# Attention loads in four transfers of 64 partitions from the nineteenth chunk on

## The chip, the cores and the metric

The kernel runs on one core of a Trainium2 chip. The metric is the device time of one execution in microseconds. Three runs of the kernel before took 819.7, 819.75 and 819.98 us; the median is 819.75 us. Its profile comes from one further execution.

## The reference

Three layers, in float32. First a decaying linear attention over 4 batches, 8 heads, 768 steps and a head size of 64:

```
state = gamma * state + outer(k[t], v[t])
y[t]  = scale * (q[t] @ state)
```

The result, 3072 tokens by 512 features, goes through `h = (x @ w1) * (x @ w2) @ w3`, `x = h @ w_out` with an inner width of 1024, and then through `h = max(x @ w1, x @ w2, x @ w3)`, `x = h @ w_out` with an inner width of 768.

## The kernel before, in words

The attention works in chunks of 128 steps: 6 chunks in each of 4 batches, 24 in all. For a chunk, TensorE multiplies k by q for each head (line 360, the scores), VectorE multiplies the scores by a mask into a buffer `a` (line 365), GpSimd multiplies v by decay factors in place (line 350, `scale_v`), and TensorE adds two parts into one PSUM bank: the state of earlier chunks times q (line 373) and the masked scores times the scaled v (line 382, `attn_av`). Line 393 adds k times v to the state. VectorE moves the result out with the output's decay factors (line 400). VectorE also copies the decay factors of each pair of chunks (line 343), and GpSimd waits for that copy.

`seq` sets the order: chunks go in pairs, one of each of two batches. Chunks 0 to 11 belong to the batches 0 and 1, chunks 12 to 23 to the batches 2 and 3. While the pair i, i+1 is in hand, the scores, masks and scaled v of the pair i+2, i+3 are made (`scores_ahead`).

A chunk arrives in one of six buffers `ck0` to `ck5`, each of 128 partitions by 4 rows of 512 floats: row 0 is q and row 1 is k with features on partitions (heads of even place on partitions 0 to 63, of odd place on 64 to 127), rows 2 and 3 are k and v with steps on partitions. `load_half(i, 0)` loads rows 0 and 1 and `load_half(i, 1)` rows 2 and 3, each by one transfer on SP's queue (line 327), 4 KB on each of 128 partitions, 512 KB. In the last chunk of a batch the second transfer is row 3 alone, 256 KB. At the end of each pair four loads for the pair six chunks ahead are written, so the loads of chunks 18 to 23 stand in the pairs that begin with 12, 14 and 16. A transfer waits for its buffer to be free and for the semaphore that it uses: the program has eight for transfers and takes them in turn, so a transfer waits until the eighth before it has landed. The order is written out by hand; no scheduler moves it.

Behind the attention, SP stores `op` buffers (line 539) and loads weights (line 93), and TensorE begins the first expert layer (lines 573 to 575).

Of the kernel before, what the change touches and what calls it, by code (L numbers as in the profile page):

```python
# [15 lines left out]
P = 128  # L16
# [3 lines left out]
CPB = S // C  # L20
# [27 lines left out]
def fused_kernel(ctx: ExitStack, tc: tile.TileContext, ck, w12, w3t, wo1, w123, wo2, mask, gout, gch, kdec, out):  # L48
    nc = tc.nc
# [261 lines left out]
    def half(hh):  # L311
        return slice(64 * hh, 64 * hh + 64)

    seq = [(2 * g + z, j) for g in range(2) for j in range(CPB) for z in range(2)]
    last = len(seq) - 1

# [3 lines left out]
    def cks(i):  # L320
        return ck_t[i % NCK]

    def load_half(i, z):
        if i <= last:
            b, j = seq[i]
            o = 3 if z and j == CPB - 1 else 2 * z
            nc.sync.dma_start(out=cks(i)[:, o:2 * z + 2, :], in_=ck[b * CPB + j, :, o:2 * z + 2, :])

    def bank4(k, n=NP):
        return bank[k].rearrange("p (n c) -> p n c", n=n)  # L330
# [87 lines left out]

    with tc.manual_schedule():
        load_half(0, 0)  # L420
        nc.scalar.dma_start(out=kdec_sb, in_=kdec)
        load_half(1, 0)
        nc.scalar.dma_start(out=mask_sb, in_=mask)
        load_half(0, 1)
        load_half(1, 1)
        nc.vector.memset(warm_sb, 0.0)
# [124 lines left out]
        for g in range(KF // GA):  # L551
            for n in range(NB):
                blk = g * NB + n
                sets = sets_b(blk)
                for q in range(7):
# [13 lines left out]
                    for p in range(GA):  # L569
# [32 lines left out]
                        z = p if blk > NB else 2 * q + p // 2  # L602
# [3 lines left out]
                    z = s - 7 * (NB - 1) - LAG  # L606
# [121 lines left out]
        for s in range(XS):  # L728
            n, r = divmod(s, 14)
# [11 lines left out]
            for m in range(2):  # L741
                ps = bank[(4 if n % 2 == 0 else 0) + (2 if which == "b" else 0) + m]
                o = slice(m * P, (m + 1) * P)
# [184 lines left out]
        for s in range(7 * NB):  # L928
            n, q = divmod(s, 7)
# [9 lines left out]
            for r in range(2):  # L939
                ps = o_sets[n % 2][which][r]  # L940
                o = slice(r * P, (r + 1) * P)
# [87 lines left out]
```

## Time and profile before

| | |
|---|---|
| time, median of three runs | 819.75 us |
| time of the profiled execution | 818.71 us |
| its span, first to last instruction | 816.4 us |
| TensorE busy in the span | 805.8 us |
| DMA, mean over the span | 302 GB/s |

The span is what the rows below count from. The profiled execution took 2.3 us more than its span. Busy time of an engine isn't what the kernel waits for: a wait matters where the chain of work that ends last runs through it. The profile gives each idle stretch of an engine a releaser, the one that came last by the profile's own times; "issue" stands where it shows none.

### The profile page before, as it was taken

The numbers are of one execution on the slowest core, as the hardware profiler recorded it, in microseconds if no ns is written. First come the engines' busy times: TensorE is split into PE (matmuls) and PEld (weight loads), VectorE is DVE, ScalarE is ACT, GpSimd is POOL, SyncE is SP. The second block draws the span as 40 slices with busy tenths as digits, with TensorE's granted clock in tenths as the row PEclk, the third lists the DMA queues.
The fourth block names the chain that finished last, engine by engine and source line by source line (L and its number), as shares of the span: only waits on it lengthen the run. The fifth ranks groups of instructions, "written<-read, shape, count | busy, mean of one in ns | idle before, by whom it ended". The sixth has DMA issues, their size and how long they took to land.

```text
span 816.4 us, 12177 instructions
## 1 busy us (share of the span) xinstructions
PE 805.8 (99%) x4648; PEld 672.6 (82%) x4648; DVE 631.4 (77%) x795; ACT 388.2 (48%) x589; POOL 74.6 (9%) x93
## 2 busy tenths in 40 slices
PE   8999999999999999999999999999999999999998
PEld 8888888888888888888888888888888888888886
DVE  3799898989598988779799839994565565688793
ACT  2442545463336454557577545453334334434642
POOL 2443000000011111001010000000000000000000
PEclk9999999999999999999999999999999999999999
DMA  9997598789999984686789798989998699956522
GB/s 346 406 408 309 212 363 342 294 336 327 371 334 416 361 327 181 217 305 214 266 300 364 260 345 308 365 297 406 409 324 304 239 336 352 321 214 216 205 104 78
DMA packets 69961, 246.55 MB, mean 302 GB/s; under 512 B 6416, under 2 KB 6544, under 8 KB 69904
## 3 DMA queue, kind: packets, MB, share of 16 engines
q1 hardware_dynamic: 48672, 165.97, 53.8%
q10 hardware_dynamic: 21232, 79.81, 27.2%
q8 instruction: 37, 0.61, 0.3%
q14 instruction: 20, 0.16, 0.0%
HBM read 163.97 MB, written 81.79 MB: 301 GB/s over the span
## 4 chain that ended last, share of the span: by engine, by line
PE 93%; DVE 0%; issue 0%; ACT 0%; ACTq 0%
PE bank L872 11%; PE bank L873 10%; PE bank L874 10%; PE bank L575 9%; PE bank L574 9%; PE bank L573 9%; PE bank L746 5%; PE bank L747 5%; PE bank L748 5%; PE bank L944 4%; PE bank L945 4%; PE bank L943 3%; PE bank L662 2%; PE bank L661 2%; PE bank L663 2%; PE abank L382 1%
## 5 line engine op out<-in xcount | busy, mean ns | idle before, releaser
L573 PE MATMUL bank<-op,w 128*128 128x512 f32 x336 | 130.8, 389 | 0.0
L575 PE MATMUL bank<-op,w 128*128 128x512 f32 x336 | 130.7, 389 | 0.0
L574 PE MATMUL bank<-op,w 128*128 128x512 f32 x336 | 130.7, 389 | 0.0
L872 PE MATMUL bank<-op,w 128*128 128x512 f32 x330 | 128.5, 389 | 0.0
L874 PE MATMUL bank<-op,w 128*128 128x512 f32 x330 | 128.4, 389 | 0.0
L873 PE MATMUL bank<-op,w 128*128 128x512 f32 x330 | 128.4, 389 | 0.0
L126 POOL TENSOR_SCALAR dec<-dec 128x512 f32<-128x512 f32 x64 | 46.6, 729 | 554.4 <-ACT dec L124 520.5
L573 PEld LDWEIGHTS bank<-op,w 128*128 128x128 f32 x336 | 63.1, 188 | 13.3 <-issue 0.2
L574 PEld LDWEIGHTS bank<-op,w 128*128 128x128 f32 x336 | 63.1, 188 | 13.2
L575 PEld LDWEIGHTS bank<-op,w 128*128 128x128 f32 x336 | 63.1, 188 | 12.9
L872 PEld LDWEIGHTS bank<-op,w 128*128 128x128 f32 x330 | 61.9, 188 | 13.5 <-ACT bank L877 0.5
L874 PEld LDWEIGHTS bank<-op,w 128*128 128x128 f32 x330 | 61.9, 188 | 13.0
L873 PEld LDWEIGHTS bank<-op,w 128*128 128x128 f32 x330 | 61.9, 188 | 12.6
L748 PE MATMUL bank<-op,w 128*128 128x512 f32 x168 | 65.4, 389 | 0.0
L746 PE MATMUL bank<-op,w 128*128 128x512 f32 x168 | 65.4, 389 | 0.0
L747 PE MATMUL bank<-op,w 128*128 128x512 f32 x168 | 65.4, 389 | 0.0
L156 ACT ACTIVATE dec<-stg 128x512 int32<-128x512 uint32 x49 | 33.1, 676 | 52.2 <-DVE stg L149 45.8
L147 DVE TENSOR_SCALAR dec<-dec 128x512 int32<-128x512 int32 x64 | 27.0, 422 | 22.7 <-POOL dec L126 22.7
L124 ACT ACTIVATE dec<-stg 128x512 f32<-128x512 f32 x49 | 32.6, 664 | 12.7 <-DMA stg<-in_w_dram 6.5
L885 DVE TENSOR_TENSOR m<-m,bank 128x512 f32<-128x512 f32 x34 | 23.3, 684 | 19.5 <-PE bank L874 18.9
L944 PE MATMUL bank<-w,wo 128*128 128x512 f32 x96 | 37.4, 390 | 0.0
L945 PE MATMUL bank<-w,wo 128*128 128x512 f32 x96 | 37.4, 389 | 0.0
(216 smaller groups left out, 1581.7 us busy)
## 6 DMA issues: line engine op xcount, KB each, us to landing
op<-opsp ACTq DMA_DIRECT2D x53, 1024.0 KB, 8.1
opsp<-op SPq DMA_DIRECT2D x34, 1024.0 KB, 5.7
ck<-in_ck_dram SPq DMA_DIRECT2D x44, 512.0 KB, 10.1
fsp<-C SPq DMA_DIRECT2D x24, 512.0 KB, 4.8
op<-opsp SPq DMA_DIRECT2D x10, 1024.0 KB, 6.0
hsp<-m SPq DMA_DIRECT2D x32, 256.0 KB, 6.0
stg<-in_w_dram SPq DMA_DIRECT2D x15, 512.0 KB, 9.3
U<-fsp SPq DMA_DIRECT2D x14, 512.0 KB, 5.9
```

What stands on the lines that cost most here:

```text
L126: nc.gpsimd.tensor_scalar(out=df, in0=df, scalar1=MAX_HI, scalar2=MIN_HI, op0=ALU.min, op1=ALU.max)
L573: nc.tensor.matmul(ps, wh, x[:, 0, k, :], start=first and k == 0 and not seeded, stop=False, skip_group_check=True)
L574: nc.tensor.matmul(ps, wh, x[:, 1, k, :], start=False, stop=False, skip_group_check=True)
L575: nc.tensor.matmul(ps, wl, x[:, 0, k, :], start=False, stop=k == 1, skip_group_check=True)
L746: nc.tensor.matmul(ps, wh, x[:, 0, k, :], start=first and kk == 0 and k == 0, stop=False, skip_group_check=True)
L747: nc.tensor.matmul(ps, wh, x[:, 1, k, :], start=False, stop=False, skip_group_check=True)
L748: nc.tensor.matmul(ps, wl, x[:, 0, k, :], start=False, stop=kk == 1 and k == 1, skip_group_check=True)
L872: nc.tensor.matmul(ps, wh, x[:, 0, k, :], start=first and k == 0 and not seeded, stop=False, skip_group_check=True)
L873: nc.tensor.matmul(ps, wh, x[:, 1, k, :], start=False, stop=False, skip_group_check=True)
L874: nc.tensor.matmul(ps, wl, x[:, 0, k, :], start=False, stop=k == 1, skip_group_check=True)
L944: nc.tensor.matmul(ps, wh[:, k, o], xl[:, k], start=False, stop=False, skip_group_check=True)
L945: nc.tensor.matmul(ps, wl[:, k, o], xh[:, k], start=False, stop=k == 2, skip_group_check=True)
```

## The change

For chunks 18 to 23 each of the two loads is cut in two by partitions, 0 to 63 and 64 to 127. That gives four transfers to a chunk instead of two, 24 instead of 12, with the same bytes. Nothing is written otherwise.

```
+    HALVES = 18
...
-            nc.sync.dma_start(out=cks(i)[:, o:2 * z + 2, :], in_=ck[b * CPB + j, :, o:2 * z + 2, :])
+            n = P if i < HALVES else P // 2
+            for r in range(0, P, n):
+                nc.sync.dma_start(out=cks(i)[r:r + n, o:2 * z + 2, :], in_=ck[b * CPB + j, r:r + n, o:2 * z + 2, :])
```

In the program after, lines behind this place have numbers four higher (line 382 becomes 386).

On SP's queue the loads of chunks 18 and 19 (buffers `ck0` and `ck1`) and the first of chunk 20 stand like this before; `DMAHW` are the eight semaphores of transfers:

```order
L327 DMA ck0_96<-in_ck_dram 128x1024 [waits DMAHW0_49]
L327 DMA ck1_97<-in_ck_dram 128x1024 [waits DMAHW1_49]
L327 DMA ck0_96<-in_ck_dram 128x1024 [waits DMAHW2_49,PE_49,Pool_49]
L327 DMA ck1_97<-in_ck_dram 128x1024 [waits DMAHW3_49,PE_49,Pool_49]
L327 DMA ck2_98<-in_ck_dram 128x1024 [waits DMAHW4_49,PE_49]
```

And now, on the same queue:

```order
L331 DMA ck0_96<-in_ck_dram 64x1024 [waits DMAHW0_49]
L331 DMA ck0_96<-in_ck_dram 64x1024 [waits DMAHW1_49]
L331 DMA ck1_97<-in_ck_dram 64x1024 [waits DMAHW2_49]
L331 DMA ck1_97<-in_ck_dram 64x1024 [waits DMAHW3_49]
L331 DMA ck0_96<-in_ck_dram 64x1024 [waits DMAHW4_49,PE_49,Pool_49]
L331 DMA ck0_96<-in_ck_dram 64x1024 [waits DMAHW5_49]
L331 DMA ck1_97<-in_ck_dram 64x1024 [waits DMAHW6_49,PE_49,Pool_49]
L331 DMA ck1_97<-in_ck_dram 64x1024 [waits DMAHW7_49]
L331 DMA ck2_98<-in_ck_dram 64x1024 [waits DMAHW0_49,PE_49]
```

Two chunks now take all eight semaphores in turn, where four chunks did. The order of the loads among each other is as it was.

On TensorE, the scores of chunks 18 and 19 and the first matmuls of line 382 for chunk 18 stand like this before:

```order
L360 MATMUL pair0_83<-ck0_96 128x128 [waits DMAHW0_49]
L360 MATMUL pair0_83<-ck0_96 128x128 x7
L360 MATMUL pair1_84<-ck1_97 128x128 [waits DMAHW1_49]
L360 MATMUL pair1_84<-ck1_97 128x128 x7
...
L382 MATMUL abank0_85<-a0_102,ck0_96 64x128 [waits DMAHW2_49,DVE_49,Pool_49]
L382 MATMUL abank0_85<-a0_102,ck0_96 64x128 x7
```

And now:

```order
L364 MATMUL pair0_83<-ck0_96 128x128 [waits DMAHW0_49]
L364 MATMUL pair0_83<-ck0_96 128x128 [waits DMAHW1_49]
L364 MATMUL pair0_83<-ck0_96 128x128 x6
L364 MATMUL pair1_84<-ck1_97 128x128 [waits DMAHW2_49]
L364 MATMUL pair1_84<-ck1_97 128x128 [waits DMAHW3_49]
L364 MATMUL pair1_84<-ck1_97 128x128 x6
...
L386 MATMUL abank0_85<-a0_102,ck0_96 64x128 [waits DMAHW4_49,DMAHW5_49,DVE_49,Pool_49]
L386 MATMUL abank0_85<-a0_102,ck0_96 64x128 x7
```

The first matmul of a chunk's scores needs the lower half of the partitions, the second the upper half, and line 382 has one more semaphore. On GpSimd, `scale_v` of these chunks likewise has one more. On VectorE and ScalarE a few instructions of the expert layer, whose buffers take over the memory of `ck`, wait for more semaphores of transfers.

## Rows read from the trace of the kernel before

**Rows 1.** The page's head: span, and TensorE's busy time, share and instructions.

```profile
span 816.4 us, 12177 instructions
...
PE 805.8 (99%) x4648; PEld 672.6 (82%) x4648; DVE 631.4 (77%) x795; ACT 388.2 (48%) x589; POOL 74.6 (9%) x93
```

**Rows 2.** TensorE's waits, whole execution: line, releaser, us, times, longest.

```profile
PE abank L382 <- POOL ck L350: 3.4, 5, 1.2
PE pair L360 <- issue: 1.5, 4, 0.5
PE abank L443 <- DVE a L426: 1.1, 1, 1.1
PE pair L360 <- DMA ck<-in_ck_dram: 0.6, 2, 0.4
PE abank L373 <- DVE xr L400: 0.2, 1, 0.2
```

**Rows 3.** Chain that ended last, 68 to 83 us: shares, then start, us, what.

```profile
by line: PE abank L382 38.0%; PE pair L360 30.7%; PE abank L373 13.8%; PE abank L393 12.4%; issue 4.7%; PE bank L573 2.9%
...
72.19 0.47 issue
...
80.98 1.90 PE abank L382 x32
82.88 0.43 PE bank L573
```

**Rows 4.** SP's queue, in order of time (start, us), then its waits to 110 us.

```profile
52.76 14.40 SPq L327 DMA_DIRECT2D ck<-in_ck_dram  x12
68.09 24.06 SPq L539 DMA_DIRECT2D opsp<-op  x3
...
SPq L327 <- DMA ck<-in_ck_dram: 26.6, 30, 2.0
```

**Rows 5.** Line 327: landing times over all loads, then four single loads.

```profile
DMA to landing us min/median/max: 4.3/10.1/11.3
...
L327 SPq DMA_DIRECT2D ck<-in_ck_dram x1: 328/328/328, 52.8 to 52.8; - x1
...
DMA to landing us min/median/max: 10.2/10.2/10.2
...
L327 SPq DMA_DIRECT2D ck<-in_ck_dram x1: 331/331/331, 55.4 to 55.4; - x1
...
DMA to landing us min/median/max: 10.1/10.1/10.1
...
L327 SPq DMA_DIRECT2D ck<-in_ck_dram x1: 328/328/328, 65.6 to 65.6; - x1
...
DMA to landing us min/median/max: 10.7/10.7/10.7
...
L327 SPq DMA_DIRECT2D ck<-in_ck_dram x1: 328/328/328, 66.8 to 66.8; - x1
...
DMA to landing us min/median/max: 10.0/10.0/10.0
```

**Rows 6.** Windows, 70 to 79 us: engines' busy us, granted clock, DMA share, GB/s.

```profile
70.00:75.00 5.00, 4.53 (x94) 4.08 (x92) 5.00 (x8) 0.96 (x2) 2.04 (x2) 1.00 1.03 402
75.00:76.00 1.00, 1.00 (x32) 1.00 (x28) 0.91 (x3) 0.00 (x0) 0.00 (x0) 1.00 0.88 354
76.00:77.00 1.00, 1.00 (x28) 1.00 (x24) 1.00 (x2) 0.37 (x1) 0.00 (x0) 1.00 0.61 238
77.00:78.00 1.00, 1.00 (x27) 0.93 (x24) 1.00 (x3) 0.43 (x2) 0.00 (x0) 1.00 0.20 74
78.00:79.00 1.00, 0.78 (x13) 0.59 (x12) 0.60 (x2) 0.88 (x1) 0.83 (x1) 1.00 0.10 41
```

**Rows 7.** GpSimd in order of time, 64 to 82 us: start, us, instructions, idle before.

```profile
66.00 2.04 POOL L350 TENSOR_TENSOR ck<-ck,kd 128x512 f32<-128x512 f32 x2 [3.78 <-DVE kd L343]
...
72.40 2.04 POOL L350 TENSOR_TENSOR ck<-ck,kd 128x512 f32<-128x512 f32 x2 [3.77 <-DVE kd L343]
78.17 2.04 POOL L350 TENSOR_TENSOR ck<-ck,kd 128x512 f32<-128x512 f32 x2 [3.73 <-DVE kd L343]
```

**Rows 8.** Line 382, 50 to 83 us: TensorE's semaphore instructions, ns min/median/max.

```profile
L382 PEldq EVENT_SEMAPHORE  x10: 51/242/754, 53.9 to 80.9; - x10
```

## Prediction

> **What bounds the kernel now.** I read the head of the page first: TensorE is busy for 805.8 of the 816.4 us span [rows 1]. So whatever the change does must pass through the 10.6 us in which TensorE is not busy, or must make some of its work late. The list of TensorE's waits, taken over the whole execution, puts all of them on lines of the attention (1.5 us are on line 360 with no releaser that the profile shows, "issue") [rows 2]. No line of the two expert layers is in the list. The chain of waits then says what the attention's tail hangs on: from 68 us to the first expert matmul at 82.88 us it is TensorE's own work throughout, but for 4.7% of "issue" [rows 3]. What comes after 82.88 us starts as late as the attention ends, with no gap that could take a delay up again. A delay at the end of the attention is therefore paid in full.
>
> Next the loads. SP's queue issues the twelve loads of chunks 18 to 23 between 52.76 and 67.16 us [rows 4]: four for each pair of chunks, first q and k of both, then k and v of both (v alone in the last pair). SP's waits on line 327 are mostly for an older load of ck, 26.6 us in 30 times [rows 4]; the order of instructions shows why, since each transfer waits for the semaphore that the eighth transfer before it used. Issue to landing, the load line's rows give 52.8 + 10.2 = 63.0 us for q and k of chunk 18, 55.4 + 10.1 = 65.5 us for k and v of chunk 18, 65.6 + 10.7 = 76.3 us for v of chunk 22 and 66.8 + 10.0 = 76.8 us for v of chunk 23 [rows 5]. Two whole transfers lie between the first two, so one of 512 KB takes about 1.27 us of the queue. The table by windows shows the queue itself full: the DMA engines' share is 1.03 at 402 GB/s from 70 to 75 us, and it falls away over the next four us (0.88, 0.61, 0.20, 0.10), so the 16 engines don't finish together [rows 6].
>
> Last, who needs the loads. GpSimd scales v by the decay (line 350), and TensorE's line 382 reads the scaled v. In the tail GpSimd's pairs of multiplies start at 66.00, 72.40 and 78.17 us, released each time by VectorE's small copy of the decays and not by a load [rows 7]. So the loads are hidden here today, and what matters is how much room they have. The last two multiplies take 2.04 us; the second of them is what chunk 23 needs. TensorE's block of 32 at 80.98 us is chunk 22 and then chunk 23, 0.95 us each, so v of chunk 23 must be scaled by 81.9 us, and must have landed by about 81.9 - 1.0 = 80.9 us. It lands at 76.8 us: room of 4.1 us.
>
> **The change part by part.** *What goes:* twelve transfers of 128 partitions. *What comes:* 24 of 64 partitions, the same bytes, in the same order. SP's twelve extra issues at 0.33 us each [rows 5] are 4 us, and lie in SP's own waits for older loads; SP's next job, the store of op at line 539, spends 24.06 us from 68.09 us mostly waiting for VectorE [rows 4]. That costs nothing.
>
> *Added waits.* On TensorE the second matmul of each chunk's scores waits for the upper half, and the first of line 382 has one semaphore more: twelve waits in six chunks. Line 382's waits stand in the trace as ten semaphore instructions with 51 ns as the shortest [rows 8]; taken at that, 12 x 0.05 = 0.6 us is the upper end, and nothing the lower end, since a wait already met may hide behind the matmuls in flight. I take 0.2 us. VectorE and ScalarE get more waits where the buffers of the expert layer take over the memory of ck, on semaphores met long before; TensorE waits for neither there [rows 2].
>
> *Rate of the halves.* This decides. No row shows a transfer that reaches fewer than 128 partitions. Lower end: the nearest row by size, v of chunk 23 (half the bytes, all 128 partitions), lands 0.5 us after its neighbour, so bytes would set the time, two halves would cost what the whole costs, and nothing would move. [...] Call s the stretch of a pair of halves against the whole, 1 to 2. The flow begins at 63.0 - 1.3 = 61.7 us and ends with v of chunk 23 at 76.8 us, 15.1 us. Then v of chunk 23 lands at 61.7 + 15.1 s, and the attention ends late by 61.7 + 15.1 s - 80.9 = 15.1 s - 19.2 us, if that is positive. It is zero at s = 1.27, and 11.0 us at s = 2. Earlier chunks are stretched less and bind less: at s = 1.6, v of chunk 19 lands after four transfers at 61.7 + 4 x 1.27 x 1.6 = 69.8 us and costs some 1.4 us, which is contained in what the last chunk costs.
>
> I take s = 1.6. The queue is full in this whole stretch, so there is no idle engine that a narrow transfer could fall back on, which speaks against the lower end. [...] The sum: 15.1 x 1.6 - 19.2 = 5.0 us, and 0.2 us of waits, is 5.2 us.
>
> [...]
>
> The profiled execution took 818.71 us, 2.3 us more than its span. With 5.2 us it comes to 823.9 us; the median of the runs shown is 819.75 us, 1.0 us above, so I forecast 825.0 us.
>
> **The rivals.** *Bytes alone set the time (s below 1.37).* Then the delay is under 15.1 x 1.37 - 19.2 = 1.5 us, and with the room of 4.1 us it is mostly none: 819.8 to 820.0 us. [...] Against it: nothing in the trace spares a full queue. This is the case on the other side, and it decides at s = 1.27.
>
> *Full price (s above 1.8).* [...] Up to 11.0 + 0.2 us: 828 to 831 us.
>
> *The window of eight.* SP keeps eight transfers in flight, now half as large. Eight of them are 8 x 0.64 = 5.1 us of the queue; if a transfer needed longer than that from issue to landing with nothing in front, the queue would run dry. The shortest landing of this line is 4.3 us, for a whole transfer at the start [rows 5]. That is below 5.1 us, so by this alone nothing runs dry; for a delay it would have to be 5.1 x 1.27 = 6.5 us. I hold it for an addition to the others at most.
>
> *Faster.* Loads release nothing in the tail, so an upper half or a lower half that lands earlier starts nothing earlier. Only the "issue" gaps could go, of which 0.47 us stands at 72.19 us [rows 3]; all four are 1.5 us.
>
> **How the numbers follow.** Within 0.2%, 1.64 us, a measurement of this kernel can't tell a change from none. My forecast (s from 1.37 to 1.8, 821.4 to 828 us) has a chance of 0.45, the full price 0.17, bytes alone with or without the window 0.35, faster 0.03. So slower has 0.62, the same 0.35, faster 0.03. The forecast's own range is 821.4 to 828 us; the range for 8 in 10 must take in the case of no change below and stops inside the full price above: 819.4 to 828.5 us.
>
> **What would show it.** Right: the loads of chunks 18 to 23 land later than now, the last near 86 us, with the DMA share full but GB/s well under 400 from 62 to 80 us; GpSimd's multiplies of the tail released by ck's DMA instead of the decays' copy; TensorE's line 382 waiting for GpSimd; the first matmul of line 577 (now 573) near 88 us, and everything after it only shifted. Wrong: GB/s stays at 400 and the first expert matmul stays at 83 us (bytes alone); or the share of the DMA engines falls below 0.9 between 62 and 75 us, which would be the window of eight and not the halves' rate.

## The result, and the profile after

The kernel after the change takes 826.28 us in the median of four runs (826.11 to 827.66), against 819.81 us before (819.7 to 819.98, again four runs): 6.5 us more. The ratio is 1.009, with a 95% interval of 1.0077 to 1.0102. It is slower by 0.9%, and the forecast was 825.0 us.

The window table of the profile after, in the columns of [rows 6] (busy us of PE, PEld, DVE, ACT and POOL, granted clock, DMA share, GB/s):

```profile
55.00:60.00 5.00, 4.57 (x90) 4.33 (x86) 4.91 (x9) 2.75 (x5) 1.05 (x2) 1.00 1.03 371
60.00:65.00 5.00, 4.18 (x98) 3.77 (x97) 3.39 (x5) 1.32 (x2) 2.68 (x3) 1.00 1.04 243
65.00:70.00 5.00, 3.96 (x66) 3.27 (x64) 4.70 (x7) 1.51 (x3) 0.00 (x0) 1.00 1.03 255
70.00:75.00 5.00, 3.45 (x74) 3.19 (x72) 2.84 (x5) 0.55 (x2) 2.66 (x3) 1.00 1.03 255
75.00:80.00 5.00, 3.64 (x72) 3.09 (x70) 5.00 (x7) 0.77 (x2) 1.04 (x1) 1.00 1.04 254
80.00:85.00 5.00, 4.18 (x84) 3.93 (x82) 3.56 (x6) 1.73 (x3) 1.04 (x1) 1.00 0.97 310
```

The DMA engines are as busy as in [rows 6], 1.03, and move 255 GB/s where they moved 402. This is the pair of numbers to look for: with the share full at the lower rate, each piece took longer, and the queue didn't wait for work. A packet of 4 KB took 261 ns in the mean from 65 to 75 us, and 163 ns in the same stretch before the change. 402 / 255 is a stretch of 1.58.

SP's queue after the change holds the load of a weight (line 93), the last whole transfer in front of the halves, and then the halves. Issue time and time to landing of that load and of four halves (lower q and k of chunk 18, upper k and v of chunk 20, of chunk 21, and upper v of chunk 23; "upper" is partitions 64 to 127):

```profile
L93 SPq DMA_DIRECT2D s_t<-in_w_dram x1: 328/328/328, 51.2 to 51.2; - x1
...
DMA to landing us min/median/max: 12.6/12.6/12.6
...
L331 SPq DMA_DIRECT2D ck<-in_ck_dram x1: 549/549/549, 52.4 to 52.4; - x1
...
DMA to landing us min/median/max: 12.4/12.4/12.4
...
L331 SPq DMA_DIRECT2D ck<-in_ck_dram x1: 466/466/466, 69.9 to 69.9; - x1
...
DMA to landing us min/median/max: 8.4/8.4/8.4
...
L331 SPq DMA_DIRECT2D ck<-in_ck_dram x1: 465/465/465, 71.9 to 71.9; - x1
...
DMA to landing us min/median/max: 8.5/8.5/8.5
...
L331 SPq DMA_DIRECT2D ck<-in_ck_dram x1: 465/465/465, 80.4 to 80.4; - x1
...
DMA to landing us min/median/max: 5.3/5.3/5.3
```

The last load lands at 80.4 + 5.3 = 85.7 us, where it landed at 76.8 us [rows 5]. The transfer of line 93 isn't cut, and yet it lands at 51.2 + 12.6 = 63.8 us. Before the change:

```profile
L93 SPq DMA_DIRECT2D s_t<-in_w_dram x1: 328/328/328, 51.5 to 51.5; - x1
...
DMA to landing us min/median/max: 10.2/10.2/10.2
```

That is 61.7 us. So 2.1 us are lost before the first half has landed.

GpSimd after the change, which answers to [rows 7] (start, us, instructions, idle before and its releaser):

```profile
70.06 1.04 POOL L354 TENSOR_TENSOR ck<-ck,kd 128x512 f32<-128x512 f32 x1 [6.08 <-DMA ck<-in_ck_dram]
72.06 1.04 POOL L354 TENSOR_TENSOR ck<-ck,kd 128x512 f32<-128x512 f32 x1 [0.96 <-DMA ck<-in_ck_dram]
...
78.50 1.04 POOL L354 TENSOR_TENSOR ck<-ck,kd 128x512 f32<-128x512 f32 x1 [4.82 <-DVE a L369]
80.88 1.04 POOL L354 TENSOR_TENSOR ck<-ck,kd 128x512 f32<-128x512 f32 x1 [1.33 <-PE abank L386]
85.17 2.04 POOL L354 TENSOR_TENSOR ck<-ck,kd 128x512 f32<-128x512 f32 x2 [3.25 <-DMA ck<-in_ck_dram]
```

Its multiplies now start when a load lands. At 78.50 and 80.88 us the row names VectorE and TensorE as the last releaser, but k and v of chunk 20 landed at 78.3 us and of chunk 21 at 80.4 us, just ahead; a wait for several semaphores is put down to one of them. In the trace the last semaphore instruction in front of these two multiplies ends at 78.41 and 80.46 us, right behind the landings. The multiply at 78.50 us begins 0.09 us after it, that at 80.88 us 0.42 us after it; what fills these 0.3 us no row shows. TensorE's waits and its matmuls that answer to [rows 2, 3]:

```profile
PE abank L386 <- POOL ck L354: 7.2, 11, 1.4
PE pair L364 <- DMA ck<-in_ck_dram: 2.4, 5, 0.7
...
PE bank L876 <- ACT bank L881: 0.9, 1, 0.9
PE pair L364 <- issue: 0.4, 1, 0.4
```

```profile
73.16 1.09 PE L386 MATMUL abank<-a,ck 128*64 128x128 f32 x16 [0.45 <-POOL ck L354]
...
79.60 1.09 PE L386 MATMUL abank<-a,ck 128*64 128x128 f32 x16 [0.84 <-POOL ck L354]
...
81.98 1.09 PE L386 MATMUL abank<-a,ck 128*64 128x128 f32 x16 [0.82 <-POOL ck L354]
...
86.82 1.97 PE L386 MATMUL abank<-a,ck 128*64 128x128 f32 x32
88.72 0.50 PE L577 MATMUL bank<-op,w 128*128 128x512 f32 x1
```

In the same view of the kernel before, line 382 begins chunks 19 and 21 and the first expert matmul starts here:

```profile
69.26 1.05 PE L382 MATMUL abank<-a,ck 128*64 128x128 f32 x16
...
75.96 1.04 PE L382 MATMUL abank<-a,ck 128*64 128x128 f32 x16
...
82.81 0.50 PE L573 MATMUL bank<-op,w 128*128 128x512 f32 x1
```

The attention ends 88.72 - 82.81 = 5.9 us late. The block of 32 at 86.82 us, which is the last pair of chunks, waited for nothing. The last wait of the attention is that at 81.98 us, for v of chunk 21.

### The profile page after: what moved, and what is told of

The parts are those of the page before. It is cut to its first block, busy times and chain, and to the rows that moved or that the text cites. A ratio compares the mean times of both kernels' runs of the same rounds, so it can differ in the third digit from the quotient of the medians.

```text
span 824.2 us, 12212 instructions
## 1 busy us (share of the span) xinstructions
PE 807.7 (98%) x4648; PEld 673.6 (82%) x4648; DVE 633.6 (77%) x795; ACT 388.3 (47%) x589; POOL 74.9 (9%) x93
## 4 chain that ended last, share of the span: by engine, by line
PE 90%; DMA 8%; DVE 1%; POOL 0%; SPq 0%; ACT 0%; issue 0%; ACTq 0%; POOLq 0%; DVEq 0%
PE bank L876 10%; PE bank L878 10%; PE bank L877 10%; PE bank L579 9%; PE bank L578 9%; PE bank L577 9%; DMA ck<-in_ck_dram 7%; PE bank L750 5%; PE bank L751 5%; PE bank L752 5%; PE bank L948 3%; PE bank L947 3%; PE bank L949 3%; PE bank L666 2%; PE bank L665 2%; PE bank L667 2%
```

## The experiments

The kernel before was run again beside the experiments, so its median differs a little from place to place. The ratios are of all runs and not of the two medians.

**By rows instead of by partitions.** As many transfers, of the same size, but each over all 128 partitions (the single row of the last chunks goes in two halves of its columns):

```
...
for r in range(o, o + 2):
    nc.sync.dma_start(out=dst[:, r, :], in_=src[:, r, :])
```

> Chunks 18 to 23 are loaded by 24 transfers of half the size again, but each over all 128 partitions: one row of the buffer (2 KB a partition) to a transfer, and two halves of the columns for the single row of the last chunks. [...] Rival N (twice as many transfers of half the size cost it: a price for each transfer, or the window of eight): 1.03 us to a transfer as after the change, attention ends near 88.8 us, 826 us. Rival X (added waits on the compute engines): also near 826 us with loads at the old rate.

Measured: 819.9 us against 819.22 us, ratio 1.0013 (1.0001 to 1.0026). The windows and the first expert matmul:

```profile
65.00:70.00 5.00, 4.24 (x94) 3.75 (x92) 4.91 (x8) 0.80 (x2) 2.67 (x3) 1.00 1.03 367
70.00:75.00 5.00, 4.47 (x94) 3.92 (x92) 5.00 (x8) 0.96 (x2) 2.09 (x2) 1.00 1.02 370
```

```profile
82.27 0.50 PE L583 MATMUL bank<-op,w 128*128 128x512 f32 x1
```

The rate is 367 to 370 GB/s, somewhat under the 402 to 410 GB/s of the kernel before in the same windows, with pieces of 2 KB instead of 4 KB, and the attention ends on time. The 0.7 us that are left are just clear of noise. Twice the number of transfers and the window of eight at half the size are out as causes of the loss. The added waits are out by the next run, where a chunk's scores and line 386 need two transfers again; here line 392, the line of the scaled v, needs row 3 alone.

**Even and odd partitions.** The transfers are again of 64 partitions and 4 KB each, but not of neighbours:

```
for r in range(n):          # n = 2 from chunk 18 on
    nc.sync.dma_start(out=cks(i)[r::n, ...], in_=ck[b * CPB + j, r::n, ...])
```

> As the change, 24 transfers of 64 partitions and 4 KB each, but the even partitions and then the odd ones, instead of 0 to 63 and 64 to 127. [...] Rival N, and a rival that any transfer of 64 partitions is slow: 255 GB/s, 826 us.

Measured: 819.1 us against 819.22 us, ratio 1.0001 (0.9992 to 1.0011). The first expert matmul:

```profile
81.54 0.50 PE L577 MATMUL bank<-op,w 128*128 128x512 f32 x1
```

From 65 to 75 us the loads run at 338 to 368 GB/s with a DMA share of 0.95 to 0.96, so here the queue isn't quite full. It isn't the number of partitions in a transfer that costs here, but which ones: 819.1 us with every second one, 826.28 us with neighbours.

**Loads alone.** Nothing but loads, twelve chunks over and over, each way of cutting between stretches of whole transfers.

> Loads alone, without the attention, the expert layers or any engine's work on the data: twelve chunks of 1 MB into twelve tiles, again and again, each way of cutting between stretches of whole transfers, and then a copy of part of it to the output. [...] Rival (a transfer of 64 partitions is slow by itself, whichever they are, or each transfer has a price): lower halves alone as fast as both in turn, and even and odd partitions and single rows as slow.

The window table of that run (POOL's busy us, clock, DMA share, GB/s): whole transfers; lower and upper halves in turn; lower halves alone; four lower and then four upper; even and odd partitions; rows:

```profile
15.00:30.00 15.00, 0.00 (x0) 1.00 1.03 410
40.00:75.00 35.00, 0.00 (x0) 1.00 1.04 243
122.00:136.00 14.00, 0.00 (x0) 1.00 1.04 205
186.00:226.00 40.00, 0.00 (x0) 1.00 1.04 220
370.00:392.00 22.00, 0.00 (x0) 1.00 1.03 408
440.00:450.00 10.00, 0.00 (x0) 1.00 1.05 375
```

Lower halves alone run at 205 GB/s, exactly half of 410. In turn they get a little back, 243 GB/s; in fours less, 220. Even and odd partitions in turn move like whole transfers, 408 GB/s, and rows at 375 GB/s. The stretch with two queues gave no answer, because ScalarE's halves ran beside whole transfers.

**Two queues, quarters, upper halves.** The two queues once more, now from the start into fresh tiles.

> Loads alone again, since the two queues of the run before overlapped with whole transfers: from the start, lower halves on SP's queue and upper halves on ScalarE's, into fresh tiles; then whole transfers, quarters of 32 partitions in turn, whole transfers, and upper halves alone. [...]

Lower halves on SP's and upper halves on ScalarE's queue; then quarters; then upper halves alone:

```profile
15.00:45.00 30.00, 0.00 (x0) 1.00 1.04 232
...
115.00:135.00 20.00, 0.00 (x0) 1.00 1.04 233
...
178.00:194.00 16.00, 0.00 (x0) 1.00 1.04 205
```

Upper halves alone move at the rate of lower ones, 205 GB/s. A second queue brings 232 GB/s, no more than one queue (243 GB/s with halves in turn).

**Chunks 18 to 21 alone.** The last pair is loaded whole again:

```
-            n = P if i < HALVES else P // 2
+            n = P if i < HALVES or i > 21 else P // 2
```

> The change for chunks 18 to 21 alone; 22 and 23 are loaded whole. From the trace after the change I now think v of chunk 21 decides (landed 80.4 us, multiplied at 80.9 us, first matmul of line 386 at 82.0 us), and the last pair has room: then the attention ends as late as after the change, 88.5 to 88.8 us, 825.5 to 826.5 us. By the prediction, in which v of chunk 23 decides, it would land some 2 us earlier and the attention would end near 86.8 us, 824.3 us.

Measured: 825.12 us against 819.22 us, ratio 1.0073 (1.0057 to 1.0089). The time lies between the two expectations, 0.4 us under mine and 0.8 us over the prediction's, so it doesn't decide; the profile does. In it line 386 begins chunk 21 at 82.28 us and the first expert matmul stands at 88.69 us, as late as with all six chunks cut:

```profile
82.28 1.09 PE L386 MATMUL abank<-a,ck 128*64 128x128 f32 x16 [1.02 <-POOL ck L354]
...
88.69 0.50 PE L577 MATMUL bank<-op,w 128*128 128x512 f32 x1
```

The granted clock of this execution was 0.50 from 68.2 to 71.6 us, but TensorE waits 1.11 us for chunk 20 and 1.02 us for chunk 21 after that, so it is the loads that set this end.

**Chunks 22 and 23 alone** (`HALVES = 22`).

> The change for chunks 22 and 23 alone. [...] Rival X (each split chunk costs by its waits): a third of the loss, 822 us.

Measured: 820.12 us against 819.22 us, ratio 1.0014 (1.0002 to 1.0025): 0.9 us. By my estimate, three whole transfers' worth of bytes stretched by 1.6 cost 0.6 x 3.85 = 2.3 us, inside the room of 4.1 us, which leaves 819.8 us within 1. The time fits that, and not the third of the loss (2.2 us) that rival X asks for. The profile that came with it is of an execution of 824.03 us and shows something else. One wait of TensorE and four windows of it:

```profile
PE pair L364 <- issue: 3.5, 3, 2.7
```

```profile
72.00:73.00 1.00, 0.00 (x0) 0.00 (x0) 1.00 (x4) 0.00 (x0) 0.59 (x1) 1.00 0.98 242
73.00:74.00 1.00, 0.00 (x0) 0.00 (x0) 0.90 (x1) 0.00 (x0) 0.79 (x2) 1.00 1.06 246
74.00:75.00 1.00, 0.33 (x3) 0.33 (x4) 0.00 (x0) 0.00 (x0) 0.70 (x1) 0.51 0.98 236
75.00:76.00 1.00, 1.00 (x11) 1.00 (x8) 0.00 (x0) 0.00 (x0) 0.00 (x0) 0.50 0.99 254
```

TensorE stands still for 2.7 us, from 71.9 to 74.7 us, in a wait without a releaser ("issue"). At 74.0 us its granted clock falls to 0.50 and stays there until about 81 us. That execution ends its attention 4.4 us late (87.17 us), and TensorE waits for nothing between 74.7 us and there, while 8 of the 10 executions of the kernel took 818.9 to 820.7 us.

**Chunks 18 and 19 alone** (`i < HALVES or i > 19` are loaded whole).

> The change for chunks 18 and 19 alone. By the trace after the change the two already cost 3.9 us where line 386 begins chunk 19, 1.4 us of which the prediction had; I put the rest on the entry: the whole transfers in front land some 2 us later too, because engines that are ahead write halves already. Then the attention ends 3.3 to 4 us late, 823 to 824 us, two thirds of the loss for a third of the split chunks. By the prediction's formula it ends 1.4 us late, 821.2 us. If each split chunk costs the same: 2 us, 821.8 us.

Measured: 824.43 us against 819.01 us, ratio 1.0064 (1.0045 to 1.0084). In its profile line 386 begins chunk 19 at 73.40 us, against 73.16 us with all six chunks cut, and the first expert matmul stands at 87.44 us, 4.6 us late:

```profile
73.40 1.09 PE L386 MATMUL abank<-a,ck 128*64 128x128 f32 x16 [0.15 <-POOL ck L354]
...
87.44 0.50 PE L577 MATMUL bank<-op,w 128*128 128x512 f32 x1
```

The two chunks cost more than I expected, and by far more than the prediction's 1.4 us. Two chunks in front cost 0.64%, two behind 0.14%, all six 0.9%: what is paid doesn't add up by chunks.

**Chunks 20 and 21 alone** (`i not in (20, 21)` are loaded whole).

> The change for chunks 20 and 21 alone. Four whole transfers' worth stretched by 1.6 is 3.1 us, and by the same entry 2 us more for the transfers in front; v of chunk 21 has room of 1.9 us. With the entry the attention ends about 3 us late, 822.5 to 823 us; without it 1.2 us late, 821 us.

Measured: 822.58 us against 819.01 us, ratio 1.0041 (1.003 to 1.0051), 3.6 us. That speaks for the entry, the 2.1 us that are lost in front of the first half: without it I had expected 821 us. Its profile doesn't settle the size, since it has a stop by "issue" of 1.93 us and the lower clock from 74.2 us on, like that of chunks 22 and 23. But that execution took 823.6 us and had a mean granted clock of 0.996. The seven of ten with 0.999 or 1.0 took 820.82 to 822.97 us, 822.32 us in the median, which is still 3.3 us more than before.

## Why the prediction was right, and where not

*What bounds, and that a delay is paid in full:* right. The attention ends 5.9 us late, and the kernel takes 6.5 us more. The two figures are of different executions: between the two profiled ones the span grew by 7.8 us (816.4 to 824.2), 1.9 us more than the delay. The stretch behind the first expert matmul took 733.6 us in the profile before and 735.5 us after; in the profiles of the other cuts it took 733.4 us (chunks 18 to 21) to 735.5 us (rows). So it takes up nothing of a delay, and it differs by 2 us between executions, whatever the cut. Part of that is a wait on line 876 (882 with rows) for ScalarE, late in the second expert layer: 0.9 us in the profile after, 0.2 us with rows, none with chunks 18 to 21.

*Rate of the halves:* right. The stretch of 1.6 was measured as 1.58, and the last load landed at 85.7 us, where 61.7 + 15.1 x 1.6 is 85.9 us. That the landing agrees to 0.2 us is in part luck. The flow of halves starts at 63.8 us and not at 61.7 us; from there to 80.4 us one whole transfer's worth takes 2.08 us, a stretch of 1.64; and the last three take 1.8 us each. The late start and the faster end cancel. The 1.6 and its upper end of 2 were estimates that no run showed when they were taken. The loads alone show 410 / 205 = 2.0 for lower halves by themselves and 410 / 243 = 1.69 for halves in turn. Why halves in turn move faster than that, and why they reach 255 GB/s in the kernel, 243 GB/s alone and 220 GB/s in fours, isn't shown: these are rates, and no row tells what limits them.

*The two halves together:* against lower halves alone (205 GB/s), the two halves moved 13% faster in a long row on two queues (232 GB/s) and 19% faster in turn on one queue (243 GB/s); even and odd partitions in turn moved at 408 GB/s.

*Which load decides:* wrong, and that the number came near is in part luck. The prediction had v of chunk 23 decide, with room of 4.1 us. It was v of chunk 21: it lands at 80.4 us instead of 73.0 us (61.7 us and the 11.3 us of its stretch, not cut), line 386 reads it at 81.98 us instead of 75.96 us, and with the last pair whole the end is the same. Its room was 1.9 us: it had to land by 75.96 - 1.04 = 74.9 us. By the prediction's own way of counting it would have been 61.7 + 11.3 x 1.6 - 74.9 = 4.9 us late, next to 5.0 us for v of chunk 23, so the two loads nearly tie and the wrong one gave a near number. I had worked out a chunk early on and the last one, and not the one between them, whose room is smaller.

*Chunk 19's cost of 1.4 us:* mis-sized. Line 386 begins chunk 19 at 73.16 us; before, its block began at 69.26 us, so it costs 3.9 us. The term left out is the entry: the whole transfer in front of the halves already lands 2.1 us late, and v of chunk 19 lands at 71.9 us, 2.1 us behind the 69.8 us of the prediction. The trace records the landing of a transfer in parts. Those of the whole one in front lie between 59.15 and 63.77 us (59.21 to 61.67 us before), and the first parts of the first and of the third half land at 60.51 and 62.68 us, so halves were under way beside it. I take it that this slows the whole one; the overlap and the landing are shown, that reason is argued.

*Waits, 0.2 us, and SP's twelve issues, nothing:* right within what can be measured: the even and odd partitions have the same number of issues and of transfers to wait for, and cost nothing (ratio 1.0001). *The window of eight:* out, by the rows: the DMA share is 1.02 to 1.03 with transfers of the same size.

No run points to a version that beats the kernel before: the cuts that cost least (ratios 1.0013 and 1.0001) also bring nothing, since no wait of the tail was for a load.

## What to carry to other kernels

Cut a transfer so that each piece still covers all of the partitions (by rows or columns), or every second one of them: here that gave ratios of 1.0013 and 1.0001. A piece of 64 neighbours moved at half the rate (205 against 410 GB/s), and a second piece or a second queue with the other half didn't make up for it (243 and 232 GB/s). Read DMA share and GB/s together: full and slow (1.03 at 255 GB/s) was the mark of it here. When a queue is full, work out the room of every load in the stretch, each against its own reader, and let the transfers in front of the change slow down too (2.1 us here).

## What I had not expected

TensorE was held up beside a full queue (DMA share 0.98 to 1.06 from 71 to 75 us) by a wait that names no load. In the profile of chunks 22 and 23 the longest "issue" wait is 2.7 us, where the kernel before has 0.5 us at the most [rows 2]. The granted clock fell from 1.00 to 0.50 while TensorE stood still, and came back 6.8 us later; from 74.7 us on TensorE was busy all that time.

What the "issue" waits are for isn't shown. The record of DMA packets has transfers of the kind "instruction" on a queue of their own (queue 8, 37 packets of 16 KB). In the kernel before, such packets end at 58.30, 64.85, 71.13 and 77.58 us, and TensorE goes on after its four "issue" waits at 59.72, 66.19, 72.67 and 79.01 us, 1.3 to 1.5 us later each time. The third of these waits, the one with chunks 22 and 23 cut and the one with chunks 20 and 21 cut all stand behind the same matmul, the 21st of the 32 scores of chunks 20 and 21; TensorE goes on at 72.67, 74.67 and 74.62 us. That the waits hang on these packets, or that the full queue lengthens them, isn't shown.

A lower clock was seen without such halves too. Of the ten executions cut by rows, three had a mean granted clock of 0.997 or 0.998 and took 821.8 to 822.7 us; the ten with even and odd partitions all had 0.999 or 1.0, and of the 39 of the kernel before beside these runs 38 had that and one 0.998, at 818.88 us. Why those three differ can't be seen, since none of them was profiled.
